# An attention and MLP kernel: one block of values and weights per head, and the remainder outputs moved to the next stage

## The chip, the cores and the metric

The kernel runs on one core of one Trainium2 chip. The metric is the device time of one execution in microseconds (us).

Engines are called PE (TensorE matmuls), PEld (TensorE weight loads), DVE (VectorE), ACT (ScalarE), POOL (GpSimd) and SP (SyncE), as in the profile.

## The reference, cut to what matters

```python
# q, k, v: 8 batches x 8 heads x 576 positions x 64;  s: 8 x 8 x 576
cum = np.cumsum(np.maximum(s, 0.0), axis=-1)
bias = -(cum[:, :, :, None] - cum[:, :, None, :])
scores = np.where(causal, -1e9, q @ k.T / 8 + np.minimum(bias, 0.0))   # causal: above the diagonal
attn = softmax(scores)                       # exp, then divided by the sum (+1e-9)
x = (attn @ v) as 4608 tokens x 512          # the 8 heads of a token side by side
out = gelu(x @ w_in) @ w_out                 # 512 -> 2048 -> 512
```

The bias is a difference of two numbers. The part that belongs to the query cancels in the softmax. The part that belongs to the key is a factor per key, the "weight". So the kernel computes P = exp(q k/8) without the bias, and for each query a numerator, the sum of P times (weight times value), and a denominator, the sum of P times weight. The attention output is numerator over denominator.

## The kernel before

The 4608 tokens are nine chunks of 512, c = 0 to 8. A chunk runs layer 1 (64 matmuls of 128x512), then layer 2 (four blocks of 16 such matmuls, one block per 128 tokens). Into layer 2 of chunk c the kernel mixes the attention of the next batch, nb = c+1: for each of the four pairs of heads the scores, then the attention outputs. A batch has 576 positions; the last 64 of them, the remainder, are kept in an accumulator of their own.

Numerators and denominators of a pair go to two accumulators in PSUM. Head 0 of the pair takes partitions 0 to 63 and head 1 takes 64 to 127, by matmuls with 64 output columns that run side by side (eight of them with 256 columns each take 0.38 us in the trace of before, 148.67 to 149.05):

```python
def av_mm(b, p, out, parts, den):
    for n_part, (jt, lo, n, off) in enumerate(parts):
        for e in range(2):
            h = 2 * p + e
            nc.tensor.matmul(
                out[e * 64 : e * 64 + 64, lo : lo + n],
                lhsT=(wb[:, jt, b * H + h : b * H + h + 1].to_broadcast([128, 64])
                      if den else vv[b % 2][:, jt, h, :]),
                rhs=P_of[b, p][:, e, off : off + n], ...)

def norm(b, p0, p1, num, den, i0, i1, chunks):           # chunks: two of 256 columns
    ln = work.tile([128, CUT], fp32, tag="ln", bufs=2, name="ln")
    for c, lo, hi in chunks:
        nc.scalar.activation(ln[:, lo:hi], den[:, lo:hi], func=AF.Ln, scale=math.exp(-LNC[c]))
    nc.scalar.activation(ln[:, :w], ln[:, :w], func=AF.Exp, scale=-1.0)     # 1 / denominator
    for c, lo, hi in chunks:
        # ... (cut: where the columns lie in xT)
        nc.vector.scalar_tensor_tensor(out, cut(num), math.exp(-LNC[c]), cut(ln), op0=MULT, op1=MULT)

def av_item(b, p, wide=False, rest=True, last=False):
    # ... (cut: other places for the accumulators in batches 0 and 1)
    num, den = [ps.tile([128, 512], fp32, tag="av", bufs=3, name=n) for n in ("avn", "avd")]
    av_mm(b, p, num, MAIN, False)
    av_mm(b, p, den, MAIN, True)
    if rest:
        av_rest(b, p)             # the remainder's numerators and denominators, tile "avr"
    norm(b, p, p + 1, num, den, 0, CUT, [(0, 0, 256), (1, 256, CUT)])
```

The tag "av" has three accumulators. Layer 2 has one, with the tag "mlp":

```python
def l2_item(c, sub, f0=0, f1=FT, av=False):
    if f0 == 0:
        tag, bufs = ("av", 3) if av else ("mlp", 1)
        o_of[c, sub] = ps.tile([128, KO * 128], fp32, tag=tag, bufs=bufs, name="o_ps")
    # ... (cut: matmuls f0 to f1 of the 16 into o_ps)
    if f1 < FT:
        return
    o_sb = work.tile([128, KO * 128], fp32, tag="osb", bufs=3, name="o_sb")
    nc.vector.tensor_copy(o_sb, o_ps)           # empties the accumulator
    nc.sync.dma_start(out=out[r0 : r0 + 128, :], in_=o_sb)
```

The order of a chunk with 1 < c < 7, after its layer 1 (`interleave`, `write_rows` and `transpose_rows` bring the queries and keys of a later batch into place by DMA):

```python
exp_set()                         # loads ScalarE's table for Exp and Ln (1.28 us in the trace)
l2_item(c, 0, 0, 4)
sc_item(nb, 0)                    # scores of pair 0: two Exps on ScalarE, masks on VectorE
l2_item(c, 0, 4)
for p in range(1, NP):
    # ... (cut: interleave, write_rows, transpose_rows)
    sc_item(nb, p)
    av_item(nb, p - 1)
    l2_item(c, p, 0, 12)
    if p == NP - 1:
        av_item(nb, p)
        norm_rest(nb)
        gelu_set()
    l2_item(c, p, 12)
```

The instructions of each engine run in the order of this program, which is scheduled by hand. What is cut: the weights, the loads, the special first chunk, and checks of the inputs with a slow path that does not run here.

## Time and profile before

| | before |
|---|---|
| time, median of 3 runs | 331.26 us (330.64 to 331.45) |
| span in the profile | 329.9 us |
| PE / DVE / ACT / POOL busy | 97% / 59% / 61% / 20% |
| one chunk, start of layer 1 to the next (chunks 2 to 6) | 34.55 us, of them layer 1 13.81 us |

These are lines of the page of before: busy time of the engines, the start of the chain of waits (work that ended last, followed back to what released it), and two groups of instructions with count, busy time, mean ns of one, and the idle time ahead of them.

```profile
PE 320.2 (97%) x2585; PEld 164.0 (50%) x2585; DVE 193.1 (59%) x384; ACT 202.8 (61%) x288; POOL 65.7 (20%) x100
...
PE 86%; DMA 9%; POOL 3%; issue 0%; DVE 0%; POOLq 0%
...
L447 DVE SCALAR_TENSOR_TENSOR xT<-avn,ln 128x256 bf16<-128x256 f32 (+3 forms) x64 | 21.7, 385 | 25.0 <-ACT ln L432 24.9
...
L431 ACT ACTIVATE ln<-avd 128x256 f32<-128x256 f32 x56 | 18.6, 391 | 12.4 <-PE avd L414 11.0
```

PE is the limit: it is busy for 97% of the span, and the chain runs through it for 86%. VectorE and ScalarE have over a third of the span free.

This is PE's timeline of before in chunk 3. The columns are start, duration and instruction; a number in brackets at the end of a line would be idle time just before it, with what ended it.

```profile
147.71 0.62 PE L376 MATMUL sc_ps<-qkT 64*128 64x256 bf16 x10
148.26 0.57 PE L414 MATMUL avn<-P,vv 128*64 128x256 bf16 x8
148.67 0.55 PE L414 MATMUL avd<-P,wb 128*64 128x256 bf16 x8
149.05 0.23 PE L414 MATMUL avr<-P,vv 128*64 128x64 bf16 x4
149.11 0.23 PE L414 MATMUL avr<-P,wb 128*64 128x64 bf16 x4
149.28 3.63 PE L514 MATMUL o_ps<-w_out_r,gT 128*128 128x512 bf16 x16
...
152.84 0.61 PE L376 MATMUL sc_ps<-qkT 64*128 64x256 bf16 x10
```

No line has brackets: PE never waits. Read the starts here, not the durations, because matmul records overlap. The 16 matmuls of layer 2 are given 3.63 us, but the scores start 3.56 us after them.

And this is the same stretch on ScalarE and on VectorE, in that order:

```profile
148.15 1.94 ACT L392 ACTIVATE P<-sc_ps 128x1024 bf16<-128x1024 f32 x2 [0.26 <-PE sc_ps L376]
149.97 0.67 ACT L431 ACTIVATE ln<-avd 128x256 f32<-128x256 f32 x2
150.67 0.63 ACT L432 ACTIVATE ln<-ln 128x512 f32<-128x512 f32 x1
```

```profile
148.40 0.68 DVE L521 COPY o_sb<-o_ps 128x512 f32<-128x512 f32 x1
...
151.33 0.76 DVE L447 SCALAR_TENSOR_TENSOR xT<-avn,ln 128x256 bf16<-128x256 f32 x2 [0.65 <-ACT ln L432]
...
152.94 0.69 DVE L521 COPY o_sb<-o_ps 128x512 f32<-128x512 f32 x1 [0.85 <-PE o_ps L514]
```

From the two Exps of a pair to the last multiply there are two Ln, an Exp and two multiplies. The multiplies end at 152.09. VectorE then waits for PE to finish the next block before it can copy it, so this side runs ahead of PE.

### The profile page before, as it was taken

The numbers are of one execution on the slowest core, as the hardware profiler recorded it, in microseconds if no ns is written. First come the engines' busy times: TensorE is split into PE (matmuls) and PEld (weight loads), VectorE is DVE, ScalarE is ACT, GpSimd is POOL, SyncE is SP. The second block draws the span as 40 slices with busy tenths as digits, with TensorE's granted clock in tenths as the row PEclk, the third lists the DMA queues.
The fourth block names the chain that finished last, engine by engine and source line by source line (L and its number), as shares of the span: only waits on it lengthen the run. The fifth ranks groups of instructions, "written<-read, shape, count | busy, mean of one in ns | idle before, by whom it ended". The sixth has DMA issues, their size and how long they took to land.

```text
span 329.9 us, 6402 instructions
## 1 busy us (share of the span) xinstructions
PE 320.2 (97%) x2585; PEld 164.0 (50%) x2585; DVE 193.1 (59%) x384; ACT 202.8 (61%) x288; POOL 65.7 (20%) x100
## 2 busy tenths in 40 slices
PE   8999999999999999999999999999999999999992
PEld 3564555445544555445544554455445544444452
DVE  5757568895669265946494748655783663150021
ACT  3897747759566857677577757677759666205400
POOL 8744243006200820710053003100000000000000
PEclk9999999999999999999999999999999999999998
DMA  7999999855975899999679655527500100010012
GB/s 113 220 209 204 207 198 254 280 91 92 251 249 115 148 260 265 178 161 228 206 147 237 178 162 131 134 105 170 137 5 34 65 35 2 32 64 32 3 64 72
DMA packets 53828, 47.30 MB, mean 143 GB/s; under 512 B 31328, under 2 KB 43872, under 8 KB 53792
## 3 DMA queue, kind: packets, MB, share of 16 engines
q0 software_dynamic: 15936, 23.07, 39.0%
q1 hardware_dynamic: 37856, 23.75, 26.8%
q8 instruction: 22, 0.36, 0.5%
q14 instruction: 14, 0.11, 0.1%
HBM read 36.85 MB, written 16.52 MB: 162 GB/s over the span
## 4 chain that ended last, share of the span: by engine, by line
PE 86%; DMA 9%; POOL 3%; issue 0%; DVE 0%; POOLq 0%
PE o_ps L514 37%; PE h_ps L495 34%; DMA w_out_r<-in_moe_w_out_dram 5%; PE sc_ps L376 5%; PE avn L414 4%; DMA w_in_r<-in_moe_w_in_dram 4%; PE avd L414 3%; PE avr L414 1%; PE o_ps L533 1%; POOL raw_v L202 1%; POOL early_k L115 1%; POOL early_q L115 1%; PE avw L414 1%; POOL w_in_r L247 0%; PE tr_ps L359 0%
## 5 line engine op out<-in xcount | busy, mean ns | idle before, releaser
L514 PE MATMUL o_ps<-w_out_r,gT 128*128 128x512 bf16 x560 | 129.4, 380 | 0.7 <-DMA w_out_r<-in_moe_w_out_dram 0.7
L495 PE MATMUL h_ps<-xT,w_in_r 128*128 128x512 bf16 x576 | 126.0, 379 | 0.6 <-DVE xT L447 0.6
L495 PEld LDWEIGHTS <-w_in_r 128*128 128x128 bf16 x576 | 56.2, 98 | 68.6 <-issue 1.0
L501 ACT ACTIVATE gT<-h_ps 128x1024 bf16<-128x1024 f32 x54 | 54.3, 1022 | 49.4 <-PE h_ps L495 49.4
L392 ACT ACTIVATE P<-sc_ps 128x1024 bf16<-128x1024 f32 x64 | 62.0, 1021 | 33.8 <-PE sc_ps L376 32.9
L514 PEld LDWEIGHTS <-gT 128*128 128x128 bf16 x560 | 51.4, 98 | 59.9 <-issue 1.0
L521 DVE COPY o_sb<-o_ps 128x512 f32<-128x512 f32 x35 | 24.0, 687 | 46.8 <-PE o_ps L514 46.7
L401 DVE TENSOR_TENSOR P<-P,tri_bf 128x512 bf16<-128x512 bf16 x58 | 23.9, 421 | 37.1 <-ACT P L392 37.0
L213 DVE TENSOR_REDUCE amx<-qkT 128x2 f32<-128x1152 bf16 x32 | 40.9, 1335 | 0.0
L447 DVE SCALAR_TENSOR_TENSOR xT<-avn,ln 128x256 bf16<-128x256 f32 (+3 forms) x64 | 21.7, 385 | 25.0 <-ACT ln L432 24.9
L202 POOL DMA_DIRECT2D raw_v<-in_v_dram x40 | 34.2, 881 | 9.6 <-DMA w_out_r<-in_moe_w_out_dram 4.2
L431 ACT ACTIVATE ln<-avd 128x256 f32<-128x256 f32 x56 | 18.6, 391 | 12.4 <-PE avd L414 11.0
L230 DVE TENSOR_TENSOR vv<-raw_v,wb 128x512 bf16<-128x512 f32 (+3 forms) x44 | 25.2, 632 | 0.7 <-DMA raw_v<-in_v_dram 0.7
L432 ACT ACTIVATE ln<-ln 128x512 f32<-128x512 f32 (+1 forms) x40 | 23.5, 587 | 1.3
L220 DVE TENSOR_REDUCE amv<-raw_v 128x1 f32<-128x2048 f32 (+1 forms) x16 | 23.0, 1471 | 1.7 <-DMA raw_v<-in_v_dram 1.7
L504 ACT ACTIVATE gT<-h_ps 128x512 bf16<-128x512 f32 x36 | 19.6, 603 | 6.3 <-PE h_ps L495 6.3
L376 PE MATMUL sc_ps<-qkT 64*128 64x256 bf16 (+2 forms) x320 | 21.4, 254 | 0.7 <-ACT P L392 0.7
L376 PEld LDWEIGHTS <-qkT 64*128 64x128 bf16 x320 | 13.3, 95 | 15.1 <-issue 12.0
L414 PEld LDWEIGHTS <-vv 128*64 128x64 bf16 x384 | 16.9, 109 | 6.8 <-issue 4.0
L414 PEld LDWEIGHTS <-wb 128*64 128x64 bf16 x384 | 17.1, 111 | 0.0
L414 PE MATMUL avn<-P,vv 128*64 128x256 bf16 x224 | 16.1, 265 | 0.0
L414 PE MATMUL avd<-P,wb 128*64 128x256 bf16 x224 | 15.4, 259 | 0.0
(94 smaller groups left out, 159.2 us busy)
## 6 DMA issues: line engine op xcount, KB each, us to landing
out_dram<-o_sb SPq DMA_DIRECT2D x35, 256.0 KB, 2.3
raw_v<-in_v_dram POOLq DMA_DIRECT2D x32, 256.0 KB, 8.7
rows<-qk_bf SPq DMA_DIRECT2D x12, 576.0 KB, 6.0
early_q<-in_q_dram POOLq DMA_DIRECT2D x14, 288.0 KB, 10.4
early_k<-in_k_dram POOLq DMA_DIRECT2D x14, 288.0 KB, 11.1
w_in_r<-in_moe_w_in_dram POOLq DMA_DIRECT2D x4, 512.0 KB, 11.5
w_out_r<-in_moe_w_out_dram POOLq DMA_DIRECT2D x4, 512.0 KB, 15.4
raw_v<-in_v_dram POOLq DMA_DIRECT2D x8, 128.0 KB, 9.9
```

The lines of the kernel that those rows point to most:

```text
L202: nc.gpsimd.dma_start(out=t[:n_st, st, :, :], in_=bass.AP(tensor=v.tensor, offset=v.offset + b * H * S * D + st * 128 * D, ap=[[D, n_st], ...
L213: nc.vector.tensor_reduce(amx[:, b * NP + p], qkT[b % 2][:, :, p, :S], axis=AX, op=ALU.max, apply_absolute_value=True)
L230: eng.tensor_tensor(vb[:n_st, st0:st1, h0:h1, :], t[:n_st, st0:st1, h0:h1, :], wb[:n_st, st0:st1, b * H + h0 : b * H + h1] .unsqueeze(3).t ...
L376: nc.tensor.matmul(s_ps[:, e, off : off + n], lhsT=qkT[b % 2][e * 64 : e * 64 + 64, 1, p, jt * 128 : jt * 128 + 128], rhs=qkT[b % 2][e * 6 ...
L392: nc.scalar.activation(P[:, :, UO[u] : UO[u] + UW[u]], s_ps[:, :, : UW[u]], func=AF.Exp, scale=scale)
L401: eng.tensor_tensor(d, d, tri_bf.unsqueeze(1).unsqueeze(1).to_broadcast([128, 2, 2, 128]), op=MULT)
L414: nc.tensor.matmul(out[e * 64 : e * 64 + 64, lo : lo + n], lhsT=(wb[:, jt, b * H + h : b * H + h + 1].to_broadcast([128, 64]) if den else ...
L432: nc.scalar.activation(ln[:, :w], ln[:, :w], func=AF.Exp, scale=-1.0)
L495: nc.tensor.matmul(h_of[c, f2][i], lhsT=w_in_r[:, ko, ft * 128 : (ft + 1) * 128], rhs=xT[:, ko, c * NB % XW : c * NB % XW + NB], start=(ko ...
L501: nc.scalar.activation(gT_of[c][:, f2 * 2 : f2 * 2 + 2, :], hh_of[c, f2], func=AF.Gelu)
L514: nc.tensor.matmul(o_ps, lhsT=gT[:, ft, sub * 128 : (sub + 1) * 128], rhs=w_out_r[:, ft, :], start=(ft == 0), stop=(ft == FT - 1),)
L521: nc.vector.tensor_copy(o_sb, o_ps)
```

## The change

The intent is to take changes of the matmul form out of PE's stream; in before, one from attention to layer 2 takes 0.11 us (layer 2 starts 0.17 us after the last four remainder matmuls, 149.11 to 149.28, and these 0.06 us after the four ahead of them). For batches 2 to 7 the 64 columns of values and the 64 columns of weights of a head become one block of 128 columns, in order values, weights for head 0 and weights, values for head 1. One matmul of 128 output columns then gives a head's numerators and denominators together, in the same full-array form as layer 2. Since the denominators of a head now lie in the other half of the partitions, each half has Ln and multiplies of its own. Only the Exp between them stays one per pair. The remainder outputs of all four pairs are computed together at the head of the next layer 2. GpSimd fills in the weights.

```diff
+    def fill_w(b):
+        for st in range(ST):
+            nc.gpsimd.tensor_copy(<the two middle 64-column parts of each pair's block>, <weights, broadcast>)

+    def vw_mm(b, p, outs, parts):
+        for e in range(2):
+            for n_part, (jt, lo, n, off) in enumerate(parts):
+                nc.tensor.matmul(
+                    outs[e][:, lo : lo + n],
+                    lhsT=vv[b % 2][:, jt, p, e * 2 * D : (e + 1) * 2 * D],
+                    rhs=P_of[b, p][:, e, off : off + n], ...)
+
+    def vw_norm(b, p0, p1, outs, i0, i1, chunks):
+        for e in range(2):
+            for c, lo, hi in chunks:
+                nc.scalar.activation(
+                    ln[e * D : e * D + D, lo:hi], outs[e][(1 - e) * D : (1 - e) * D + D, lo:hi],
+                    func=AF.Ln, scale=math.exp(-LNC[c]))
+        nc.scalar.activation(ln[:, :w], ln[:, :w], func=AF.Exp, scale=-1.0)
+        for e in range(2):
+            r = slice(e * D, e * D + D)
+            # ... one multiply per chunk of columns on the partitions r alone

     def av_item(...):
-        av_mm(b, p, num, MAIN, False)
-        av_mm(b, p, den, MAIN, True)
-        if rest:
-            av_rest(b, p)
-        norm(b, p, p + 1, num, den, 0, CUT, [(0, 0, 256), (1, 256, CUT)])
+        # batches 0 and 1 as before, without av_rest; the others:
+        vw_mm(b, p, (num, den), MAIN)
+        vw_norm(b, p, p + 1, (num, den), 0, CUT, [(0, 0, 256), (1, 256, CUT)])

         # chunk c, layer 2
             exp_set()
             l2_item(c, 0, 0, 4)
-            if c == 1:
-                for p in range(NP):
-                    av_rest(1, p)
+            for p in range(NP):
+                av_rest(c, p)
             sc_item(nb, 0)
-            if c == 1:
-                norm_rest(1)
+            norm_rest(c)
             l2_item(c, 0, 4)
...
                     av_item(nb, p)
-                    norm_rest(nb)
                     gelu_set()
```

Cut from the diff: chunk 7 gets the remainder of batch 7 at its head. In chunk 0 the first layer-2 blocks swap places, so that the last part of w_out is wanted later. A few warm-up matmuls become shorter, the buffers for raw values go from three to two, and one check of the values moves ahead of a load.

More of the change, by code (lines that the diff above doesn't have):

```diff
@@ L153 @@
     w_out_r = const.tile([128, FT, KO * 128], bf16, name="w_out_r")
-    vv = [const.tile([128, ST, H, D], bf16, name=f"vv{i}") for i in range(2)]
+    vv = [const.tile([128, ST, NP, 4 * D], bf16, name=f"vv{i}") for i in range(2)]
     qkT = [const.tile([128, 2, NP, 640], bf16, name=f"qkT{i}") for i in range(2)]
@@ L197, in load_v @@
         if (b, "v") not in raws:
-            raws[b, "v"] = work.tile([128, ST, H, D], fp32, tag="rawv", bufs=3, name="raw_v")
+            raws[b, "v"] = work.tile([128, ST, H, D], fp32, tag="rawv", bufs=2, name="raw_v")
         t = raws[b, "v"]
@@ L229, in scale_v @@
             n_st = 128 if st1 < ST else SL
-            eng.tensor_tensor(
-                vb[:n_st, st0:st1, h0:h1, :],
-                t[:n_st, st0:st1, h0:h1, :],
-                wb[:n_st, st0:st1, b * H + h0 : b * H + h1]
-                .unsqueeze(3).to_broadcast([n_st, st1 - st0, h1 - h0, D]),
-                op=MULT,
+            if h1 - h0 == 2:
+                eng.tensor_tensor(
+                    vb[:n_st, st0:st1, h0 // 2, :].rearrange("j s (x d) -> j s x d", d=D)[:, :, 0:4:3],
+                    t[:n_st, st0:st1, h0:h1, :],
+                    wb[:n_st, st0:st1, b * H + h0 : b * H + h1]
+                    .unsqueeze(3).to_broadcast([n_st, st1 - st0, 2, D]),
+                    op=MULT,
+                )
+                continue
+            for st in range(st0, st1):
+                eng.tensor_tensor(
+                    vb[:n_st, st, h0 // 2 : h1 // 2, :].rearrange("j p (x d) -> j p x d", d=D)[:, :, 0:4:3],
+                    t[:n_st, st, h0:h1, :].rearrange("j (p e) d -> j p e d", e=2),
+                    wb[:n_st, st, b * H + h0 : b * H + h1].rearrange("j (p e) -> j p e", e=2)
+                    .unsqueeze(3).to_broadcast([n_st, (h1 - h0) // 2, 2, D]),
+                    op=MULT,
+                )
+    def fill_w(b):
+        for st in range(ST):
+            nc.gpsimd.tensor_copy(
+                vv[b % 2][:, st, :, D : 3 * D].rearrange("j p (e d) -> j p e d", d=D),
+                wb[:, st, b * H : (b + 1) * H].rearrange("j (p e) -> j p e", e=2)
+                .unsqueeze(3).to_broadcast([128, NP, 2, D]),
             )
@@ L417, in av_mm @@
                         wb[:, jt, b * H + h : b * H + h + 1].to_broadcast([128, 64])
-                        if den else vv[b % 2][:, jt, h, :]
+                        if den else vv[b % 2][:, jt, p, e * 3 * D : e * 3 * D + D]
                     ),
@@ L450, in norm, with av_item @@
                     )
-    def av_item(b, p, wide=False, rest=True, last=False):
+    def av_item(b, p, wide=False, last=False):
         if wide:
@@ L460, in av_item @@
             num, den = [ps.tile([128, 512], fp32, tag="av", bufs=3, name=n) for n in ("avn", "avd")]
-        av_mm(b, p, num, MAIN, False)
-        av_mm(b, p, den, MAIN, True)
-        if rest:
-            av_rest(b, p)
-        norm(b, p, p + 1, num, den, 0, CUT, [(0, 0, 256), (1, 256, CUT)])
+        if b < 2:
+            av_mm(b, p, num, MAIN, False)
+            av_mm(b, p, den, MAIN, True)
+            norm(b, p, p + 1, num, den, 0, CUT, [(0, 0, 256), (1, 256, CUT)])
+            return
@@ new lines, in av_item @@
+        vw_mm(b, p, (num, den), MAIN)
[6 more added lines that the diff above has]
+                    lhsT=vv[b % 2][:, jt, p, e * 2 * D : (e + 1) * 2 * D],
+                    rhs=P_of[b, p][:, e, off : off + n],
+                    start=(n_part == 0), stop=n_part == len(parts) - 1,
+                    skip_group_check=True,
+                )
@@ new lines, in vw_norm, with cut @@
+    def vw_norm(b, p0, p1, outs, i0, i1, chunks):
+        ln = work.tile([128, CUT], fp32, tag="ln", bufs=2, name="ln")
+        w = (p1 - p0) * (i1 - i0)
+        for e in range(2):
+            for c, lo, hi in chunks:
+                nc.scalar.activation(
+                    ln[e * D : e * D + D, lo:hi], outs[e][(1 - e) * D : (1 - e) * D + D, lo:hi],
+                    func=AF.Ln, scale=math.exp(-LNC[c]),
+                )
+        nc.scalar.activation(ln[:, :w], ln[:, :w], func=AF.Exp, scale=-1.0)
+        for e in range(2):
+            r = slice(e * D, e * D + D)
+            for c, lo, hi in chunks:
+                a = i0 if p1 - p0 > 1 else i0 + lo
+                z = i1 if p1 - p0 > 1 else i0 + hi
+                t0 = (b * S + a) % XW
+                for u0, u1 in ((0, min(z - a, XW - t0)), (XW - t0, z - a)):
+                    if u0 < u1:
+                        x0 = (t0 + u0) % XW
+                        def cut(t):
+                            t = t[r, lo:hi].rearrange("d (p i) -> d p i", p=p1 - p0)
+                            return t[:, :, u0:u1] if p1 - p0 > 1 else t[:, 0, u0:u1]
+                        o = xT[r, p0:p1, x0 : x0 + u1 - u0]
+                        nc.vector.scalar_tensor_tensor(
+                            o if p1 - p0 > 1 else o[:, 0], cut(outs[e]), math.exp(-LNC[c]), cut(ln),
+                            op0=MULT, op1=MULT,
+                        )
@@ L469, in av_rest @@
             rest_of[b] = ps.tile([128, 2, NP, SL], fp32, tag="av", bufs=3, name="avr")
+        parts = [(jt, 0, n, off) for jt, n, off in REST]
+        if b > 1:
+            vw_mm(b, p, [rest_of[b][:, e, p] for e in range(2)], parts)
+            return
         for den in range(2):
-            av_mm(b, p, rest_of[b][:, den, p], [(jt, 0, n, off) for jt, n, off in REST], den)
+            av_mm(b, p, rest_of[b][:, den, p], parts, den)
     def norm_rest(b):
         t = rest_of[b].rearrange("d n p i -> d n (p i)")
-        norm(b, 0, NP, t[:, 0], t[:, 1], CUT, S, [(2, 0, NP * SL)])
+        if b > 1:
+            vw_norm(b, 0, NP, (t[:, 0], t[:, 1]), CUT, S, [(2, 0, NP * SL)])
+        else:
+            norm(b, 0, NP, t[:, 0], t[:, 1], CUT, S, [(2, 0, NP * SL)])
     gT_of = {}
@@ L557, with keep_busy @@
     warm = ps.tile([128, 512], fp32, tag="mlp", bufs=1, name="warm")
-    def keep_busy(n):
+    def keep_busy(n, w=512):
         for _ in range(n):
-            nc.tensor.matmul(warm, lhsT=busy[:, :128], rhs=busy, start=True, stop=True)
+            nc.tensor.matmul(warm[:, :w], lhsT=busy[:, :128], rhs=busy[:, :w], start=True, stop=True)
     weights_scan()
@@ L567 @@
     weights_dve()
-    keep_busy(3)
+    keep_busy(3, 256)
     sc_item(0, 0, masks=False)
     tr_item(0, 1, 0)
-    keep_busy(1)
+    keep_busy(1, 256)
     tr_item(0, 1, 1)
@@ L602 @@
     for p in range(NP):
-        av_item(0, p, wide=p < 2, rest=False, last=p == 3)
+        av_item(0, p, wide=p < 2, last=p == 3)
     gelu_set()
@@ L622 @@
                 absmax(c, p)
+        if 1 < c and nb < B:
+            nc.gpsimd.tensor_copy(pace, gT_of[c][:, 0, 0:1])
+            fill_w(nb)
         if 1 < c and nb + 1 < B:
-            nc.gpsimd.tensor_copy(pace, gT_of[c][:, 0, 0:1])
             load_v(nb + 1)
@@ L640 @@
             norm_rest(0)
+            fill_w(2)
             sc_item(1, 0)
+            l2_item(c, 1, 0, 8, av=True)
+            sc_item(1, 1)
             l2_item(c, 0, 8)
-            sc_item(1, 1)
-            l2_item(c, 1, 0, 8, av=True)
             tr_item(1, 2, 0)
@@ L651 @@
             sc_item(1, 2)
-            l2_item(c, 2, 0, 8)
+            l2_item(c, 2, 0, 8, av=True)
             scale_pair(1, 1)
             sc_item(1, 3)
-            l2_item(c, 2, 8)
+            l2_item(c, 2, 8, av=True)
             scale_pair(1, 2)
-            av_item(1, 0, rest=False)
+            av_item(1, 0)
             scale_pair(1, 3)
-            av_item(1, 1, wide=True, rest=False)
+            av_item(1, 1, wide=True)
             l2_item(c, 3, 0, 8)
@@ L662 @@
             write_rows(2, 0, nc.sync)
-            av_item(1, 2, wide=True, rest=False)
+            av_item(1, 2, wide=True)
             l2_item(c, 3, 8)
@@ L666 @@
             write_rows(2, 1, nc.sync)
-            av_item(1, 3, rest=False)
+            av_item(1, 3)
             for p in (0, 1):
@@ L672 @@
                 transpose_rows(2, p)
+            absmax_v(1)
             nc.gpsimd.tensor_copy(pace, qkT[0][:, 1, 3, 0:1])
@@ L675 @@
             load_v(3)
-            absmax_v(1)
         elif nb < B:
@@ L715 @@
                 cert_1()
+                exp_set()
+                for p in range(NP):
+                    av_rest(c, p)
+                norm_rest(c)
+                gelu_set()
             for sub in range(4):
```

## The prediction

It was written with the code of both kernels and the profile of before at hand, before the changed kernel had run.

> **What bounds it now.** TensorE. The table of engines has PE busy 97%, and in the chain of waits PE holds 86%; from 41.57 to 324 us it is PE without a break. One steady stage (batch 3, chunk 3 in the timeline of PE) takes 34.55 us: 13.81 us of layer 1, then 20.74 us in which layer 2 is mixed with scores and attention outputs of the next batch. A 512-column matmul costs 0.216 us there, so that part needs 13.8 us of layer 2, 1.7 us of scores and 3.4 us of attention outputs: 18.9 us. The missing 1.8 us is mostly some 0.11 us at each change between full-array, row-tiled (scores) and column-tiled (attention) matmuls, 13 in a stage: the same 8 attention matmuls take 0.50 us after such a change and 0.38 us without. [...]
>
> **What the change does.**
> - Streaming columns stay equal: before, two 64-column matmuls ran side by side (0.38 us for numerators, 0.38 us for denominators); now eight 128-wide ones run one after another (estimate 0.75 us). What goes is the changes between attention output and layer 2: 5 a stage, 0.55 us, and 0.36 us of remainders moves to the head.
> - ScalarE: four Ln per pair instead of two (x2 takes 0.67 us, x4 by estimate 1.23 us). VectorE: four multiplies per pair instead of two (0.76 to about 1.45 us). GpSimd: five fills per batch, by the memset slopes about 0.65 us each, close to the path in chunk 2 alone, where the queue is late.
> - Remainders at the head of layer 2: their Ln, Exp and multiplies come, in VectorE's order, ahead of the copy that empties layer 2's only accumulator. The Exps of the first pair end 4.5 us after layer 2's start (table load first). Then two Ln 0.67, Exp 0.45, two multiplies 0.76, copy 0.68 us: the accumulator comes free about 7.0 us after layer 2's start, where PE wants it at about 6.2 us. It now starts there at 5.93 us. So I expect a new PE wait of 0.6 to 1.0 us in each of chunks 2 to 6, against 0.8 us that the stage saves later.
> - The longer chain Exps, Ln, Exp, multiplies, copy also becomes nearly as long as PE's period for pairs 2 and 3: up to 0.2 us of wait each.
> - Start: the reordered chunk 0 removes the 0.68 us wait for the last part of w_out; the shorter warm-up matmuls give about 0.4 us.
>
> **Sum.** Start -1.0; chunk 1 -0.4; chunks 2 to 6 +0.4 each, +2.0; chunk 2's fills +0.3; remainders in chunk 7 +0.5. About +1.2 us: **332.4 us**, 8 in 10 between 329.4 and 335.0. Faster by over 2%: 4%; within 2%: 91%; slower: 5%.
>
> **What would show it.** PE's wait ahead of the second layer-2 block, named after the copy of the output tile, 0.6 to 1.0 us in chunks 2 to 6; wait for w_out gone; attention blocks followed by layer 2 with no extra 0.11 us; ScalarE and VectorE up about 15 us each, 288 matmuls fewer.
>
> **What would make it wrong.** If that wait is not there, all 0.7 us a stage is gained: about 326 us. If GpSimd's fills are over 1 us [...], chunk 2 and the masks slip: 335 us.

The 0.11 us and the 0.38 us are in the trace of before. 0.50 us is there as 0.48 to 0.51, for eight attention matmuls with the change behind them (54.04 to 54.52, 20.28 to 20.79); with the change ahead of them they take 0.41 (148.26 to 148.67). The memset slopes can be read from two MEMSETs on GpSimd in the same trace, 0.101 us for 128x1 and 0.335 us for 128x256: 0.92 ns a column, or 0.57 us for 512 columns (estimate), a little under the text's 0.65.

## More of the kernel before

`LNC` holds fixed scales. So a denominator's accumulator is free after the Ln, and a numerator's after the multiply.

## The result, and the profile after

| | before | after |
|---|---|---|
| time, median of 4 runs each on one chip | 331.05 us (330.64 to 331.45) | 342.63 us (342.01 to 343.81) |
| ratio, with 95% interval | | 1.0354 (1.0323 to 1.0385), slower |
| span in the profile | 329.9 us | 340.8 us |
| chunk 1, chunk 2 | 35.02, 34.56 us | 36.72, 36.99 us |
| each of chunks 3 to 6 | 34.55 us | 36.22 us (chunk 4: 36.29) |

A ratio is the mean time of one kernel's fast runs over that of the other's in the same rounds, so it is not quite the ratio of the medians in the table. Chunk times run from the start of a layer 1 to the start of the next, read from PE's timeline.

The page of after, the lines that answer to those of before, and the group of GpSimd's fills:

```profile
PE 317.7 (93%) x2297; PEld 161.0 (47%) x2297; DVE 220.9 (65%) x446; ACT 224.8 (66%) x344; POOL 90.3 (26%) x131
...
PE 53%; DMA 14%; POOL 10%; ACT 9%; issue 8%; DVE 4%; SPq 0%; POOLq 0%; DVEq 0%
...
L523 DVE SCALAR_TENSOR_TENSOR xT<-avn,ln 64x256 bf16<-64x256 f32 (+3 forms) x56 | 18.4, 372 | 26.4 <-ACT ln L507 26.4
...
L250 POOL COPY vv<-wb 128x512 bf16<-128x512 bf16 x30 | 24.0, 854 | 0.0
...
L503 ACT ACTIVATE ln<-avn 64x256 f32<-64x256 f32 x48 | 15.6, 374 | 6.1 <-PE avn L490 5.6
...
L523 DVE SCALAR_TENSOR_TENSOR xT<-avd,ln 64x256 bf16<-64x256 f32 (+3 forms) x56 | 19.0, 386 | 0.7
```

There are 288 matmuls fewer and PE is busy 2.5 us less, but its share falls from 97% to 93%, and the chain leaves PE for nearly half of the span. A multiply on 64 partitions takes 0.37 to 0.39 us, where one on 128 took 0.39 (means over several widths). A Ln on 64 partitions takes 0.374 us, where one on 128 took 0.391. So twice as many instructions are nearly twice the time: ScalarE is busy 22 us more and VectorE 28 us. Neither is near being full, at 66% and 65%.

The view of all waits in after has two new lines for PE (total us, times, longest):

```profile
PE o_ps L582 <- DVE o_sb L589: 9.4, 12, 1.3
...
PE avd L490 <- DVE xT L523: 2.1, 6, 0.6
```

PE's timeline of after in chunk 3 shows where they lie. Layer 2 begins at 147.05.

```profile
147.05 1.03 PE L582 MATMUL o_ps<-w_out_r,gT 128*128 128x512 bf16 x4
147.91 0.63 PE L490 MATMUL avr<-P,vv 128*128 128x64 bf16 x16
...
152.66 0.55 PE L490 MATMUL avd<-P,vv 128*128 128x256 bf16 x4
154.49 3.61 PE L582 MATMUL o_ps<-w_out_r,gT 128*128 128x512 bf16 x16 [1.29 <-DVE o_sb L589]
...
158.98 0.55 PE L490 MATMUL avd<-P,vv 128*128 128x256 bf16 x4
159.36 3.62 PE L582 MATMUL o_ps<-w_out_r,gT 128*128 128x512 bf16 x16
...
163.85 0.55 PE L490 MATMUL avd<-P,vv 128*128 128x256 bf16 x4
164.77 2.75 PE L582 MATMUL o_ps<-w_out_r,gT 128*128 128x512 bf16 x12 [0.38 <-DVE o_sb L589]
167.36 0.55 PE L490 MATMUL avn<-P,vv 128*128 128x256 bf16 x4
168.22 0.54 PE L490 MATMUL avd<-P,vv 128*128 128x256 bf16 x4 [0.31 <-DVE xT L523]
```

A chunk has three stops. The second layer-2 block and the fourth wait for the copy that empties layer 2's only accumulator. The second half of pair 3 waits for an accumulator of pair 2. It starts at 168.22, after the multiplies that read pair 2's "avn" (they end at 168.07) and before those that read "avd" (168.10 to 168.87, below). The names have stayed: "avn" is now the accumulator of head 0, "avd" that of head 1. Before, the denominators' accumulator was free after the Ln; now neither is.

The stops cost more than the brackets say. Without a stop, layer 2 starts 0.38 us after "avd" (158.98 to 159.36). At 154.49 it starts 1.83 us after it, so the stop costs 1.45 us against 1.29 in brackets. The other two cost 0.54 and 0.48. The brackets count from the modelled end of the last matmul, and that is later than the time at which the next could have started: a layer-2 matmul is recorded with 0.379 us but follows the last one after 0.216 (the 64 of layer 1 take 13.81 us). The difference of 0.163 us is what the stops cost beyond their brackets, 0.16 to 0.17 us each. The three stops together delay a chunk by 2.47 us.

ScalarE and VectorE of after in the same stretch:

```profile
149.65 1.94 ACT L410 ACTIVATE P<-sc_ps 128x1024 bf16<-128x1024 f32 x2
151.61 0.77 ACT L503 ACTIVATE ln<-avr 64x256 f32<-64x256 f32 x2
152.41 0.42 ACT L507 ACTIVATE ln<-ln 128x256 f32<-128x256 f32 x1
152.73 1.92 ACT L410 ACTIVATE P<-sc_ps 128x1024 bf16<-128x1024 f32 x2
154.68 0.65 ACT L503 ACTIVATE ln<-avn 64x256 f32<-64x256 f32 x2
155.35 0.64 ACT L503 ACTIVATE ln<-avd 64x256 f32<-64x256 f32 x2
156.03 0.63 ACT L507 ACTIVATE ln<-ln 128x512 f32<-128x512 f32 x1
```

```profile
152.86 0.86 DVE L523 SCALAR_TENSOR_TENSOR xT<-avr,ln 64x256 bf16<-64x256 f32 x2 [0.68 <-ACT ln L507]
153.75 0.69 DVE L589 COPY o_sb<-o_ps 128x512 f32<-128x512 f32 x1
...
156.69 0.75 DVE L523 SCALAR_TENSOR_TENSOR xT<-avn,ln 64x256 bf16<-64x256 f32 x2 [0.58 <-ACT ln L507]
157.47 0.77 DVE L523 SCALAR_TENSOR_TENSOR xT<-avd,ln 64x256 bf16<-64x256 f32 x2
158.26 0.69 DVE L589 COPY o_sb<-o_ps 128x512 f32<-128x512 f32 x1
...
167.32 0.75 DVE L523 SCALAR_TENSOR_TENSOR xT<-avn,ln 64x256 bf16<-64x256 f32 x2 [1.44 <-ACT ln L507]
168.10 0.77 DVE L523 SCALAR_TENSOR_TENSOR xT<-avd,ln 64x256 bf16<-64x256 f32 x2
```

The first stop is the chain 151.61 to 154.44: Ln of the remainder, Exp, two multiplies, and only then the copy, although PE had finished the block to be copied two microseconds earlier (scores at 151.72). PE starts 0.05 us after the copy ends. For pair 0 the four Ln take 1.31 us (154.68 to 155.99), where before two took 0.67, and the multiplies take 1.55 us (156.69 to 158.24), where they took 0.76.

The stop ahead of the fourth block can be read in the same way. Its chain begins with the scores that start at 158.04, and nothing is handed on to it from the pair before: ScalarE waits 1.82 us for these scores. The multiplies end 5.96 us after the scores start (164.00), the copy ends at 164.72 and PE starts at 164.77. PE by itself gets from the scores to that block in 6.19 us (e9_ln_halves below, where it does not stop there).

Chunk 2 has one thing of its own. This is VectorE and then GpSimd of after at its head:

```profile
113.72 2.87 DVE L419 TENSOR_TENSOR P<-P,tri_bf 128x512 bf16<-128x512 bf16 x2 [3.15 <-ACT P L410]
```

```profile
113.25 3.05 POOL L250 COPY vv<-wb 128x512 bf16<-128x512 bf16 x5
```

Two masks that take 0.42 us each elsewhere take 2.87 us together, and the second ends when GpSimd's five fills end, to 0.3 us (116.59 and 116.30). How the fills hold up the masks, no trace shows; that they do is tried in e5_fill_early below, where the fills lie elsewhere and chunk 2 falls from 36.99 to 36.23 us.

Where the 10.8 us of span come from, as differences of chunk times: start of the kernel -0.43; chunk 1 +1.70; chunk 2 +2.43; chunks 3 to 6 +1.67, +1.73, +1.66, +1.67; from chunk 7 on +0.40.

### The profile page after: what moved, and what is told of

The parts are those of the page before. It is cut to its first block, busy times and chain, and to the rows that moved or that the text cites. A ratio compares the mean times of both kernels' runs of the same rounds, so it can differ in the third digit from the quotient of the medians.

```text
span 340.8 us, 5974 instructions
## 1 busy us (share of the span) xinstructions
PE 317.7 (93%) x2297; PEld 161.0 (47%) x2297; DVE 220.9 (65%) x446; ACT 224.8 (66%) x344; POOL 90.3 (26%) x131
## 4 chain that ended last, share of the span: by engine, by line
PE 53%; DMA 14%; POOL 10%; ACT 9%; issue 8%; DVE 4%; SPq 0%; POOLq 0%; DVEq 0%
PE h_ps L563 27%; PE o_ps L582 20%; DMA early_k<-in_k_dram 7%; DMA w_in_r<-in_moe_w_in_dram 4%; POOL raw_v L202 4%; ACT P L410 3%; ACT ln L503 2%; DMA qkT<-rows 2%; DVE xT L523 2%; POOL vv L250 2%; PE sc_ps L394 1%; ACT gT L572 1%; DVE o_sb L589 1%; PE avd L490 1%; DMA early_q<-in_q_dram 1%
## 5 line engine op out<-in xcount | busy, mean ns | idle before, releaser
L582 PEld LDWEIGHTS <-gT 128*128 128x128 bf16 x560 | 52.9, 98 | 69.1 <-issue 11.0
L419 DVE TENSOR_TENSOR P<-P,tri_bf 128x512 bf16<-128x512 bf16 x58 | 25.5, 457 | 24.0 <-ACT P L410 23.1
L523 DVE SCALAR_TENSOR_TENSOR xT<-avn,ln 64x256 bf16<-64x256 f32 (+3 forms) x56 | 18.4, 372 | 26.4 <-ACT ln L507 26.4
L692 POOL CAST pace<-gT 128x1 f32<-128x1 bf16 x5 | 2.6, 513 | 92.6 <-ACT gT L569 92.6
L490 PEld LDWEIGHTS <-vv 128*128 128x128 bf16 x288 | 19.9, 98 | 10.5 <-PE avn L490 3.3
L240 DVE TENSOR_TENSOR vv<-raw_v,wb 128x512 bf16<-128x512 f32 (+2 forms) x36 | 23.7, 715 | 1.2 <-DMA raw_v<-in_v_dram 1.0
L250 POOL COPY vv<-wb 128x512 bf16<-128x512 bf16 x30 | 24.0, 854 | 0.0
L503 ACT ACTIVATE ln<-avn 64x256 f32<-64x256 f32 x48 | 15.6, 374 | 6.1 <-PE avn L490 5.6
L523 DVE SCALAR_TENSOR_TENSOR xT<-avd,ln 64x256 bf16<-64x256 f32 (+3 forms) x56 | 19.0, 386 | 0.7
L507 ACT ACTIVATE ln<-ln 128x512 f32<-128x512 f32 (+1 forms) x30 | 17.6, 587 | 1.0
```

The costliest lines, as they stand in the source:

```text
L240: eng.tensor_tensor(vb[:n_st, st, h0 // 2 : h1 // 2, :].rearrange("j p (x d) -> j p x d", d=D)[:, :, 0:4:3], t[:n_st, st, h0:h1, :].rearra ...
L250: nc.gpsimd.tensor_copy(vv[b % 2][:, st, :, D : 3 * D].rearrange("j p (e d) -> j p e d", d=D), wb[:, st, b * H : (b + 1) * H].rearrange("j ...
L419: eng.tensor_tensor(d, d, tri_bf.unsqueeze(1).unsqueeze(1).to_broadcast([128, 2, 2, 128]), op=MULT)
L523: nc.vector.scalar_tensor_tensor(o if p1 - p0 > 1 else o[:, 0], cut(outs[e]), math.exp(-LNC[c]), cut(ln), op0=MULT, op1=MULT,)
L582: nc.tensor.matmul(o_ps, lhsT=gT[:, ft, sub * 128 : (sub + 1) * 128], rhs=w_out_r[:, ft, :], start=(ft == 0), stop=(ft == FT - 1),)
```

## The experiments

The theory after reading the result: the passes on half of the partitions lengthen the chain on ScalarE and VectorE that frees accumulators, and PE waits for accumulators. The rivals were that the new place of the remainder does it, that the wide matmuls themselves do, that the new start or GpSimd's fills do, and that ScalarE starts its Ln late because they cross partitions. All times are against before on the same chip in the same rounds; "chunk" is the steady chunk, 34.55 us in before and 36.22 in after.

### e1_copy_first: after, with the remainder's multiplies behind the copy

```diff
-            norm_rest(c)
             l2_item(c, 0, 4)
+            norm_rest(c)
```

> The changed kernel, with only the normalisation of the remainders moved behind the rest of the first layer-2 block in program order, so that VectorE empties layer 2's accumulator before it multiplies the remainders. Theory (the order on VectorE makes PE wait 1.3 us before the second layer-2 block in chunks 2 to 6): that wait falls under 0.2 us, the chunk period of chunks 3 to 6 falls from 36.2 to about 35.1 us, the whole from 342.6 to 337 us (335.5 to 338.5). Rival (ScalarE and VectorE just have too much to do in the stage, wherever the copy stands): the wait moves to the later blocks and the time stays within 1.5 us of 342.6.

Measured: 341.02 us (339.86 to 342.39, 4 runs), ratio 1.027 (1.022 to 1.032). The chunk is 35.87 us. PE's timeline of this run has, in chunk 3:

```profile
160.09 3.61 PE L582 MATMUL o_ps<-w_out_r,gT 128*128 128x512 bf16 x15 [0.89 <-DVE o_sb L589]
...
168.94 0.54 PE L490 MATMUL avd<-P,vv 128*128 128x256 bf16 x4 [0.84 <-DVE xT L523]
```

The stop ahead of the second block is gone, and the time comes back at the third block and at pair 3. My expectation of 337 us fell, and the rival held in the main: the wait moves on (its time, within 1.5 us of 342.6, is just missed, by 0.1). The order at the head alone is not the cause; the whole chain from pair to pair is too long.

### e2_halves: before, with Ln and multiplies in halves

Nothing else is changed: the matmuls keep their 64 columns, and the remainders their place.

```diff
-        for c, lo, hi in chunks:
-            nc.scalar.activation(ln[:, lo:hi], den[:, lo:hi], func=AF.Ln, ...)
+        halves = [slice(0, 128)] if b < 2 else [slice(0, 64), slice(64, 128)]
+        for r in halves:
+            for c, lo, hi in chunks:
+                nc.scalar.activation(ln[r, lo:hi], den[r, lo:hi], func=AF.Ln, ...)
...             # and the multiplies likewise
```

> The kernel before, matmuls untouched, with Ln and the multiplies of batches 2 to 7 each done in two halves of 64 partitions, as the change does. Theory (the doubled instruction count is what costs, through the accumulators it holds longer): PE waits for the multiplies at the attention outputs of pair 3, over 1 us a chunk, and the time rises by 5 to 9 us, to 336 to 340 us. Rival (the remainders' new place is what costs, the halves are hidden): under 333 us.

Measured: 339.40 us (338.58 to 341.24, 4 runs), ratio 1.023 (1.018 to 1.028). The chunk is 35.76 us (chunks 5 and 6; 35.85 and 35.90 in 3 and 4), with one stop in PE's timeline:

```profile
165.75 0.57 PE L414 MATMUL avd<-P,wb 128*64 128x256 bf16 x8 [1.01 <-DVE xT L449]
```

Half passes alone, on the old matmuls, cost about two thirds of the loss. The theory held.

### e3_rest_head: before, with the remainder at the head

```diff
-        if rest:
-            av_rest(b, p)
...
-            if c == 1:
-                for p in range(NP):
-                    av_rest(1, p)
+            for p in range(NP):
+                av_rest(c, p)
...             # norm_rest(c) after sc_item(nb, 0), as in the change; old matmul form and whole passes
```

> The kernel before, with only the remainders of every batch moved to the head of the next layer 2, in their old form (64 columns, whole-partition Ln and multiply). Theory: the copy that empties the accumulator just fits, as it does in chunk 1 of the kernel before; 330 to 332.5 us. Rival (the new place itself costs, in any form): over 335 us.

Measured: 334.75 us (333.25 to 336.92, 4 runs), ratio 1.008 (1.003 to 1.014). The chunk is 34.61 us in chunks 4 to 6, 0.05 above before, and the part from chunk 7 on is 0.7 us longer. Chunk 3 of the profiled run, its slowest, has a wait for a DMA that transposes queries and keys, which the others do not have (that DMA is on the chain that ended last for 16.12 us, from 139.79 to 155.91, and VectorE then stands idle for 2.84 us until 157.45); the chunk takes 39.11 us. What makes the other three runs, at 333.25 to 334.86 us, slower than before was not traced. Neither expectation was met exactly. The place of the remainder is worth 0.05 us a chunk while the passes are whole, so it is no cause by itself.

### e4_start: before, with the changed start

```diff
-            l2_item(c, 0, 8)
+            l2_item(c, 1, 0, 8, av=True)
             sc_item(1, 1)
-            l2_item(c, 1, 0, 8, av=True)
+            l2_item(c, 0, 8)
...             # and the shorter warm-up matmuls
```

> The kernel before, with only the start of the change: shorter warm-up matmuls, and chunk 0's second output tile ahead of the second half of the first. Theory: the 0.68 us wait for w_out goes, and DMA of batch 1 takes some of it back: 0.3 to 0.8 us faster, 330.2 to 330.8 us. Rival (other waits take all of it): within 0.2 us of before.

Measured: 333.07 us (332.30 to 333.75, 4 runs), ratio 1.003 (0.998 to 1.007). The wait for w_out is gone, and PE waits for the queries and keys of batch 1 instead (0.40 and 1.41 us in this trace). The start gains nothing, and my expectation fell; the median is 1.5 us above before, more than the rival's 0.2, but the ratio's interval includes 1. What was waited for was the loads as a whole.

### e5_fill_early: after, with the fill for batch 3 a chunk earlier

```diff
-            fill_w(nb)
+            if c > 2:
+                fill_w(nb)
...
                     if c == 1:
+                        fill_w(3)
```

> The changed kernel with the fills for batch 3 issued in chunk 1 ahead of the pacing copy, instead of at the head of chunk 2's layer 2. Theory [...]: chunk 2 falls from 37.0 to about 36.2 us as the other chunks, the masks fall from 2.87 us for two to under 1.4 us, the whole about 0.7 us faster than the change, 341 to 342 us. Rival (fills cost nothing): within 0.3 us of the change in that chunk.

Measured: 342.80 us (342.19 to 343.50, 4 runs), ratio 1.033 (1.028 to 1.037). Chunk 2 falls from 36.99 to 36.23 us, as forecast, and PE's waits for its masks (0.55 and 0.37 us in after, up to 115.90 and 116.64) are gone, so the fills over the masks are what set chunk 2 apart, by 0.76 us. The whole, forecast at 341 to 342, is no faster than after's 342.63: the profiled spans are 340.4 and 340.8 us. In this trace layer 1 of chunk 1 starts 1.4 us later than in after's (60.93 against 59.53), and chunk 1 takes 35.68 us against 36.72. So the first 96 us differ from run to run by as much as the fill is worth.

### e6_whole: after, with whole passes; wrong result

The wide matmuls, fills and remainder place of after, but Ln and multiplies on 128 partitions as before. Half of the rows are then no denominators, so an Exp that stays finite stands where the Ln were.

```diff
-        vw_norm(b, p, p + 1, (num, den), 0, CUT, ...)
+        norm(b, p, p + 1, num, den, 0, CUT, ...)
...
+            if b > 1:
+                nc.scalar.activation(ln[:, lo:hi], den[:, lo:hi], func=AF.Exp, scale=1e-30)
```

> The changed kernel with the normalisation of batches 2 to 7 back to whole-partition instructions: two first ScalarE passes, one Exp and two multiplies per pair, as in the kernel before. The result is wrong on purpose (the denominators are not where it reads them), and an Exp of a tiny multiple stands for Ln so that nothing becomes infinite; matmuls, fills and places are those of the change. Theory (the doubled half-partition passes are the cost, the 128-wide matmuls gain): chunk period of chunks 4 to 6 at 33.9 to 34.3 us, no wait over 0.3 us there, the whole at 329 to 332 us. Rival (the wide matmuls, the fills or the new place cost by themselves): chunk period over 35 us, the whole over 336 us.

Measured: 330.09 to 332.22 us in three fast runs (a fourth, 335.60, was slow and is left out), ratio 0.997 (0.990 to 1.003). The chunk is 34.14 us with one stop left:

```profile
151.37 3.61 PE L585 MATMUL o_ps<-w_out_r,gT 128*128 128x512 bf16 x16 [0.21 <-DVE o_sb L592]
```

With the same matmuls as after the chunk loses 2.08 of its 36.22 us, and is 0.41 us faster than before. The matmuls are not the cause; the half passes are, with what they hold: this kernel also frees the denominators' accumulator after its first pass, as before did. In whole-kernel time this is level with before.

### e7_halves_head: before, with half passes and the remainder at the head

The edit is that of e2_halves and that of e3_rest_head together.

```diff
+        halves = [slice(0, 128)] if b < 2 else [slice(0, 64), slice(64, 128)]
...
+            for p in range(NP):
+                av_rest(c, p)
```

> The kernel before with both the halves of e2 and the new place of e3, matmuls still 64 columns wide, no fills. Theory: the third accumulator is free at pair 3, but the copy that empties layer 2's accumulator now comes late: PE waits about 1.0 us at the second layer-2 block and under 0.6 us at pair 3; chunk period 36.0 to 36.6 us, near that of the change although its matmuls are the old ones; 339 to 343 us. Rival (freeing the third accumulator takes e2's loss away): period under 35.3 us, under 336 us.

Measured: 339.52 us (338.25 to 340.58, 4 runs), ratio 1.022 (1.016 to 1.027). The chunk is 35.66 us in chunks 5 and 6 (35.88 and 35.80 in 3 and 4), up to 0.3 under what I expected; the time lies in the range. The stop is now 0.97 us ahead of the second layer-2 block, where the prediction had put it, and there is none at pair 3. Compared with e2_halves, the place of the remainder moves the stop but hardly changes its size.

### e8_ln_own_half: after, with Ln that stay in their own half

In after, ScalarE starts the Ln 0.02 us after the Exps end (151.59 to 151.61). In before it starts them 0.12 us ahead of that end (150.09 to 149.97). If the crossing of halves is the reason, then Ln that read and write the same partitions should win this back; the multiply crosses instead.

```diff
-                    ln[e * D : e * D + D, lo:hi], outs[e][(1 - e) * D : ..., lo:hi],
+                    ln[(1 - e) * D : (1 - e) * D + D, lo:hi], outs[e][(1 - e) * D : ..., lo:hi],
```

> The changed kernel, in which each Ln writes the same 64 partitions that it reads, and the multiply takes its second operand from the other half, instead of the Ln crossing halves. Theory (part of the error of the forecast is that a crossing Ln does not overlap with the instruction before it on ScalarE): Ln starts before the Exp ahead of it has ended, as in the kernel before (0.12 us), the waits at the copies shrink by 0.1 to 0.2 us each, chunk period 35.7 to 36.1 us, the whole 1 to 2.5 us faster than the change. Rival (the lost overlap has another cause): chunk period 36.2 us as in the change.

Measured: 341.21 us (340.67 to 343.47, 4 runs), ratio 1.031 (1.024 to 1.038). The chunk is 36.22 us, to the hundredth that of after, and Ln still starts 0.02 us late. The whole is 1.4 us less than after's, but on another chip, and the intervals of the ratios overlap. This theory fell: crossing is not what holds the Ln back. The traces show another condition. e8_ln_own_half still reads the upper half first. e2_halves reads the lower half first, and there the Ln start ahead of the end of the two Exps (at 152.05), as in before:

```profile
151.93 1.30 ACT L433 ACTIVATE ln<-avd 64x256 f32<-64x256 f32 x4
```

This is so in the seven traces whose ScalarE was read, in chunks 2 to 6 of before and after and in chunk 3 of the others. Where the first Ln reads partition 0 onwards (before, e2, e9, e10), it starts 0.11 to 0.12 us ahead of the end of the Exps; where it reads partition 64 onwards (after, e8, e11), 0.02 us behind it. The few that start later wait for something else. The same happens at each later switch of half in after: the second pair of Ln starts 0.02 us behind the first pair, the second pair of multiplies and the copy 0.01 to 0.03 us behind what is ahead of them, where two Ln on one half overlap by 0.10 us and two multiplies by 0.08. That makes some 0.5 us in the chain of a pair (estimate: 0.14 + 0.12 + 0.11 + 0.11). No run varied the order of the halves on purpose.

### e9_ln_halves and e10_mul_halves: e6_whole, with one of the two in halves; wrong results on purpose

```diff
+        for r in (slice(0, 64), slice(64, 128)):           # e9: the stand-in for Ln in halves
+            for c, lo, hi in chunks if b > 1 else []:
+                nc.scalar.activation(ln[r, lo:hi], den[r, lo:hi], func=AF.Exp, scale=1e-30)
```

> e6 (wrong on purpose) with the first ScalarE passes of batches 2 to 7 in two halves again, multiplies whole. The chunk period tells which engine's doubling costs how much of the 2.1 us between e6 (34.14) and the change (36.2). Theory (both engines lie in one chain, so each half of the doubling costs about its own length): 34.7 to 35.3 us. Rival (VectorE's queue alone is the cost): within 0.2 us of 34.14.

```diff
+        halves = [slice(0, 128)] if b < 2 else [slice(0, 64), slice(64, 128)]
-        for c, lo, hi in chunks:                           # e10: the multiplies in halves
+        for r, c, lo, hi in [(r, *x) for r in halves for x in chunks]:
```

> e6 (wrong on purpose) with the multiplies of batches 2 to 7 in two halves again, first ScalarE passes whole. Theory (one chain): chunk period 34.8 to 35.4 us. Rival (ScalarE's passes alone are the cost): within 0.2 us of 34.14.

Measured: 333.07 and 335.08 us, one run each, so their state is unknown and only the chunks are used. The chunk is 34.51 us with Ln in halves (0.37 above e6_whole) and 34.70 us with the multiplies in halves (0.56 above), both a little under my ranges. Each has one stop, ahead of the second block, of 0.58 and 0.77 us. Together that is 0.93 us, but after is 2.08 above e6_whole. The stops at the fourth block and at pair 3 appear in neither.

For the fourth block the reason is slack. From the start of the scores to the end of the multiplies it takes 4.38 us in e6_whole, 5.01 with Ln in halves, 5.15 with the multiplies in halves and 5.96 in after. PE wants that block 6.19 us after the scores, and the copy and its hand-over take 0.77 of them, so about 5.42 us are free. Either half of the work fits, and both do not. Pair 3 is another matter. In e7_halves_head, with both doublings, its "avd" starts at 166.43 while the four multiplies of pair 2 still run (166.02 to 167.55): PE does not wait for them, because the denominators' accumulator was free after the Ln. So the stop of after at pair 3 comes from accumulators that are held until their multiplies. In e2_halves it came from the remainder's accumulator, which is in use through the whole chunk.

### e11_reordered: after, with its instructions in another order

The same work and the same result as after. The copy goes ahead of the remainder's multiplies. For pairs 0 and 1 the layer-2 copy goes between the two halves of the multiplies, and the scores of pair 3 are started inside the block of pair 2, so that ScalarE gets them earlier. The fill for batch 3 goes a chunk earlier.

```diff
             sc_item(nb, 0)
-            norm_rest(c)
             l2_item(c, 0, 4)
+            norm_rest(c)
...
-                sc_item(nb, p)
-                av_item(nb, p - 1)
-                l2_item(c, p, 0, 12)
+                if p < NP - 1:
+                    sc_item(nb, p)
+                rest_mul = av_item(nb, p - 1, split=p < NP - 1)   # second half of the multiplies kept back
+                if p == NP - 2:
+                    l2_item(c, p, 0, 8)
+                    sc_item(nb, p + 1, masks=False)
+                    l2_item(c, p, 8, 12)
+                else:
+                    l2_item(c, p, 0, 12)
...
                 l2_item(c, p, 12)
+                if p < NP - 1:
+                    rest_mul()
+                if p == NP - 2:
+                    # the masks of pair 3
```

> The changed kernel with the same instructions in another order: layer 2's accumulator is copied out between the two halves of the multiplies and ahead of the remainders, the scores of pair 3 are computed half a block earlier, and batch 3's fills come earlier. Theory (the loss is in what the accumulators wait for, not in the amount of work on any engine): no PE wait over 0.4 us in chunks 3 to 6, period 33.9 to 34.6 us, the whole 329 to 333 us, so level with the kernel before or a little better. Rival (ScalarE and VectorE can't carry the doubled passes at that pace): period over 35.5 us, the whole over 337 us.

Measured: 331.48 us (328.56 to 332.34, 5 runs), ratio 1.001 (0.995 to 1.006), correct. The chunk is 34.12 us. PE's timeline of this run around pairs 2 and 3 of chunk 3 has no brackets:

```profile
151.94 0.54 PE L490 MATMUL avd<-P,vv 128*128 128x256 bf16 x4
152.44 1.89 PE L588 MATMUL o_ps<-w_out_r,gT 128*128 128x512 bf16 x8
154.26 0.61 PE L394 MATMUL sc_ps<-qkT 64*128 64x256 bf16 x10
...
160.46 0.55 PE L490 MATMUL avd<-P,vv 128*128 128x256 bf16 x4
```

All 11 us come back with ScalarE and VectorE still busy 69% and 67% of the span. So it was the order of the work and what it holds, and not its amount.

### e12_old_start: e11_reordered, with the start of before

The question was whether a version beats both kernels, since e11_reordered gains 0.43 us in each of four chunks.

```diff
-            l2_item(c, 1, 0, 8, av=True)
+            l2_item(c, 0, 8)
             sc_item(1, 1)
-            l2_item(c, 0, 8)
+            l2_item(c, 1, 0, 8, av=True)
...             # and the full warm-up matmuls
```

> The reordered kernel of e11 with the start of the kernel before (longer warm-up, old order of chunk 0's layer 2), since over nine traces with the new start the second layer 1 begins at 60.3 us on the average and at 59.9 us over the four with the old one. Theory: chunk periods as in e11 (34.1 us), the whole 329.5 to 331 us, ratio to the kernel before 0.993 to 1.000. Rival (the new start is worth something in most executions): slower than e11's ratio of 1.0006.

Measured: 332.55 us (331.42 to 333.98, 6 runs), ratio 1.001 (0.997 to 1.005) against before at 331.79 (331.05 to 334.17, 11 runs). It is level, and 1.5 us over my range. Chunks 3 to 6 give 34.12 to 34.18 us, but chunk 2 takes 35.51 and the part from chunk 7 on is 0.40 us longer than in before. No version that ran is clearly faster than before.

### One sum for the steady chunk

If PE's stops are all that differs among the kernels with wide matmuls, then a chunk is a fixed time, plus the idle time in brackets, plus 0.17 us for each stop. The fixed time is worked out from e6_whole: 34.14 - 0.21 - 0.17 = 33.76 us.

| kernel | idle in brackets, chunk 3 or 6 | sum | measured |
|---|---|---|---|
| after | 1.29 + 0.38 + 0.31 | 36.25 | 36.22 |
| e1_copy_first | 0.89 + 0.84 | 35.83 | 35.87 |
| e9_ln_halves | 0.58 | 34.51 | 34.51 |
| e10_mul_halves | 0.77 | 34.70 | 34.70 |
| e11_reordered | none | 33.76 | 34.12 |

Before's 34.56 with the stop of e2_halves, 1.01 + 0.17, gives 35.74, where 35.76 was measured. The 0.36 us left in e11_reordered are stops too short to show. A stop of less than the 0.16 us by which matmul records overlap leaves no bracket. In its timeline above, layer 2 starts 0.50 us after "avd" where 0.38 is usual; the next block does so after 0.56 us, and "avd" itself starts 0.46 us after "avn" where 0.39 is usual. That is 0.37 us in all. Both blocks start within 0.06 us of the end of a copy by VectorE (152.39 and 157.43), as the stops of after do.

## Why the prediction was wrong

It said 332.4 us, 329.4 to 335.0, with 91% for a change within 2%. The kernel takes 342.63 us and is 3.5% slower. Its first wait was forecast in the right place; the size of the waits, and what the last one is for, were not.

- **What bounds the kernel.** Right: PE, with the part of layer 2 where it is mixed with attention as the place of the change.
- **What PE gains.** Right. "0.8 us that the stage saves later" is 34.56 - 33.76 = 0.80 us of the sum above. After the wide matmuls layer 2 starts at once (158.98 to 159.36, 0.38 us), without the extra 0.11 us that before had there (in e3_rest_head, with the old matmuls and no remainder in between, it starts after 0.48 us). Why the change of form costs this, no trace shows.
- **The first stop.** Right place, too small. The text put the release "about 7.0 us after layer 2's start, where PE wants it at about 6.2 us"; it came after 7.44 us, and PE wanted it after 5.99. The remainder's two Ln took 0.77 us for 0.67, the multiplies 0.86 for 0.76, and the Ln started after the Exps instead of overlapping them (the switch of half, see e8_ln_own_half). So the stop delays PE by 1.45 us, where "0.6 to 1.0" was expected.
- **The failed step** is this one: "The longer chain Exps, Ln, Exp, multiplies, copy also becomes nearly as long as PE's period for pairs 2 and 3: up to 0.2 us of wait each." The chain did not become nearly as long, but longer: 6.73 us from the scores to the start of the fourth block, against PE's 6.19. Its stops cost 0.54 us at the fourth block and 0.48 us at pair 3, and the second of these was not for the copy at all. It was for an accumulator of pair 2, which the change keeps until its multiplies, and which the prediction does not mention. The prediction had counted four Ln and four multiplies per pair correctly. What it had too short were these passes at a switch of half: four Ln took 1.31 us for 1.23, four multiplies 1.55 for 1.45, and the Ln began 0.14 us later behind the Exps than before. So a steady chunk missed the forecast by 1.27 us, about half at the first stop (1.45 where the middle of the range was 0.8) and half at these two (1.02 where 0.4 was allowed).
- **The sum of a chunk.** The text has "chunks 2 to 6 +0.4 each", from stops of about 1.2 us less 0.8. Measured are 2.47 less 0.80, that is +1.67 us. Over five chunks this is 6.3 of the 9.4 us that the forecast terms missed. (The terms add up to +1.4, where the text says about +1.2.)
- **Chunk 2's fills.** "+0.3" was +0.76, by e5_fill_early. That the masks slip was named as a risk: two took 2.87 us while the fills ran. A fill takes 0.654 us in the median, as estimated; the mean of 0.854 comes from a few, up to 1.53 us.
- **Chunk 1.** "-0.4" was +1.70, the largest miss in one chunk. Batch 2 goes through the half passes there already, and has three stops (0.30, 0.62 and 0.96 us in brackets). The text had counted the gain there and no stop. One of them lies behind a VectorE copy that started at 88.03, a microsecond later than in before, because the load of those queries was issued a microsecond later (80.15 against 79.19; both landed after 7.8 us). Chunk 1 differs from run to run: e8_ln_own_half, with nearly the instructions of after, took 36.01 us in it, and e5_fill_early 35.68. How much of the 1.70 us is stops and how much loads was not tried apart, nor was the cut from three buffers for raw values to two.
- **Start.** "-1.0" was -0.43 in the trace, and e4_start shows no gain in time: the wait passes from one load to another.
- **End.** "+0.5" was +0.40. About right.
- **Engine totals.** "About 15 us each" more for ScalarE and VectorE was 22 and 28. The figures per pair, 0.56 us more Ln and 0.69 us more multiplies, make 13 and 17 us over 24 pairs. The extra passes of the six remainders, the table loads of 1.28 us that chunk 7 now needs and the slower masks were left out.

What was shown: half passes alone on the old kernel lose 8 us (e2_halves), whole passes on the new one lose nothing (e6_whole), and another order of the same instructions wins the loss back (e11_reordered). What stays open is how much of the loss the switches of half make by themselves, since no run changed them alone, and the exact parts of chunk 1.

## What to carry to other kernels

When PE is the limit, an engine at 65% can still set the pace, by holding the accumulators that PE needs next. So before a change that adds passes there, write down for each accumulator when it is released and when PE wants it again, counted from the matmuls that start its chain, and look for accumulators that the change holds longer. A pass over half of the partitions cost here as much as a whole one (256 columns on 64 and on 128 partitions: a Ln 0.374 and 0.391 us in the mean, a multiply 0.405 to 0.429 and 0.415 to 0.425 us in chunk 3), and a switch between halves lost 0.11 to 0.14 us against the overlap without one, so count passes and switches and not elements, and order the work so that what frees an accumulator comes first.
